# Attention and two feed-forward layers on one core: the second layer's second product of batches 2 and 3 from seven block products for eight, and due times shifted by kind of step and stage

## The chip, the cores and the metric

The kernel runs on one core of one Trainium2 chip. The metric is the device time of one execution in microseconds (us). Before the change the median of three timed runs is 1192.38 us (1186.67, 1192.38 and 1195.06).

## The reference

Attention with normalised queries and keys over 4 batches, 12 heads, 448 positions, head size 64; its output, put together to 1792 tokens by 768, goes through two feed-forward layers, each 768 to 2048 and back to 768, all in float32:

```
attn = softmax(rmsnorm(q) @ rmsnorm(k).T / 8) @ v
x = attn as [1792, 768]
h = x @ w_in;    x = (silu(h)) @ w_out          # first layer
h = x @ w2_in;   out = (relu(h) ** 2) @ w2_out  # second layer
```

## The kernel before, in words

The engines are named as in the profile: PE multiplies matrices, DVE, ACT and POOL work elementwise, SP issues the DMAs.

**Precision.** A float32 operand is split into an upper part in PE's fast format (a cast, kinds of step ending in `_hi`) and the rest (a subtraction, `_lo`). Each product is three matmuls: upper by upper, and the two of upper by lower. The casts stand at L523 (ACT) and L525 (DVE), the subtractions at L532 (DVE or POOL).

**Second layer** (`layer2`). It runs over two halves, each two batches: 896 tokens. In each half a loop over eight groups `fg` of 256 of the 2048 hidden features; one pass is called a slot here. The slot's first product, 768 to 256, is made from seven block products for eight (`seven`): the input halves B11 to B22 are combined beforehand (T1 to T4, B21, tiles `raw`, `yb`, `xb`, `part`), the weights too (w0, a22, z, v_, tiles `w` and `v`). Each of the products P1 to P7 is 9 matmuls of 448 columns (L1075) into a bank of the rings "t" (3 banks) or "pv" (1). DVE adds them up (`plus`, L1090) in the four buffers of ring `g`; ACT applies relu (L1338), DVE, ACT or POOL the square (L1344, L1346), and the result is split into `gh` and `gl`. The four blocks of it are named by (feature block, batch): (0,0), (0,1), (1,0), (1,1).

The second product takes 7 chunks of 128 tokens by two halves of 384 outputs. Each of these 14 is 6 matmuls of 384 columns (L1367) into a bank of ring "s", which has four; then ACT copies the bank into `total` in the first slot (L1388) or DVE adds it (L1394, "accumulate" below), tile `gg` in the profile. After the last slot each chunk is stored.

**What sets the order.** A planner (`Plan`) records all steps with each engine's cost for them, lists them by a simulated run forward, takes a due time for each from a run backward, and repeats this 8 times (`schedule`); between steps that could start at the same time the earlier due time goes first. Every engine then issues its steps in the order found. In half 1 (the second half, batches 2 and 3) the weights of the first product come ready split from DRAM (`w<-su`, `sw`, `sz`, `sv`, `v<-sa`, L927), each 768 KB (`sa` 384 KB). In the trace half 0 has its slots up to about 937 us, its accumulates to about 985 us beside the start of half 1, which ends with the kernel.

Of the kernel before, what the change touches and what calls it, by code (L numbers as in the profile page):

```python
# [8 lines left out]
F32 = mybir.dt.float32  # L9
# [6 lines left out]
P = 128  # L16
# [5 lines left out]
NQ = 4  # L22
# [6 lines left out]
SEVEN = (1,)  # L29
SEGS = [(h, n) for h in range(2) for n in range(NQ)]  # L30
# [81 lines left out]
AHEAD = 25.0  # L112


class Plan:
# [233 lines left out]
    def schedule(self):  # L349
# [7 lines left out]
        while todo:  # L357
            n = todo.pop()
            e = at[n]
            t, xfer, _ = steps[n].on[e]  # L360
            due[n] -= t + (xfer or 0.0) + LAG[e]
            for m, timed in self.pre[n]:
                due[m] = min(due[m], due[n])
                seen[m] -= 1
                if not seen[m]:
                    todo.append(m)
        best = None
        got = [None]
        for _ in range(ROUNDS):
# [4 lines left out]
            due = [-x for x in late]  # L374
# [14 lines left out]
def kernel(  # L389
# [674 lines left out]
    def seven(x, w, at, finish):  # L1064
# [36 lines left out]
        plus(u3, u2, p7)  # L1101
        p4 = psum("t")
# [5 lines left out]
        p5 = psum("t")  # L1108
        product(p5, z, 0, "T1")
        plus(u3, u3, p5)  # L1110
        finish(1, 1, u3)
        plus(u2, u2, p5)
# [201 lines left out]
    def layer2():  # L1314
# [3 lines left out]
        SLOT = 7 * PROD + TC * DOWN2  # L1318
        for half in range(2):
            t = half * NG * SLOT  # L1320
            x = second_x(half, ("end", t - 60.0), ("end", t - 20.0))
            total = sb([P, TC, DM], F32, "gg", 1, "yp")
            for fg in range(NG):
                f0, f1 = 2 * fg, 2 * fg + 1
                at = ("end", t)
# [5 lines left out]
                gl = sb([P, 2, 2 * S], FR, "gl", 1, "yp")  # L1331

                def finish(fi, bi, g, src=None, gh=gh, gl=gl):

                    k = slice(bi * S, (bi + 1) * S)
# [6 lines left out]
                    def square(e):  # L1342
# [5 lines left out]
                    step("square", at, {**any_t(S), **act_t(S)}, square, writes=[g])  # L1348
                    split(
                        ("h_hi", "h_lo"), at, lambda: gh.ap[:, fi, k], lambda: gl.ap[:, fi, k], lambda: g.ap,  # L1350
                        [g], [(gh, (fi, bi)), (gl, (fi, bi))],
                    )

                seven(x, w, ("end", t), finish)
                t += 7 * PROD

                for tc_ in range(TC):
                    bs = range(tc_ * P // S, ((tc_ + 1) * P - 1) // S + 1)
                    for nh in range(2):
                        pt = psum("s")  # L1360

                        def products(e, gh=gh, gl=gl, wo=wo, tc_=tc_, pt=pt, nh=nh):
                            n = 0
                            for fi in range(2):
                                _, _, wh, wl = wo[fi]
                                for w_, g in ((wh, gh), (wl, gh), (wh, gl)):
                                    nc.tensor.matmul(  # L1367
                                        pt.ap[:, :NH],
                                        g.ap[:, fi, tc_ * P:(tc_ + 1) * P],
                                        w_()[:, 0, nh * NH:(nh + 1) * NH],  # L1370
                                        start=(n == 0),
                                        stop=(n == 5),
                                    )
                                    n += 1

                        step(
                            "down2", ("end", t), pe_t(DOWN2 / 2), products,
                            reads=[z for w in wo for z in w[:2]]
                            + [(z, (fi, bi)) for z in (gh, gl) for fi in range(2) for bi in bs],
                            writes=[pt],  # L1380
                        )

                        def o(tc_=tc_, nh=nh, total=total):
                            return total.ap[:, tc_, nh * NH:(nh + 1) * NH]

                        if fg == 0:
                            step(
                                "acc", ("end", t), act_t(NH), lambda e, o=o, pt=pt: nc.scalar.copy(o(), pt.ap[:, :NH]),  # L1388
                                reads=[pt], writes=[(total, (tc_, nh))],
                            )  # L1390
                        else:
                            step(
                                "acc", ("end", t), dve_t(NH),
                                lambda e, o=o, pt=pt: nc.vector.tensor_tensor(o(), pt.ap[:, :NH], o(), ALU.add),  # L1394
                                reads=[pt], writes=[(total, (tc_, nh))],
                            )
                        t += DOWN2 / 2
                    if fg == NG - 1:

                        r0 = tc_ * P  # L1400
                        while r0 < (tc_ + 1) * P:
                            g_, t0_ = divmod(r0, CP)
                            r1 = min((tc_ + 1) * P, (g_ + 1) * CP)
# [3 lines left out]
                                lambda e, total=total, tc_=tc_, r0=r0, r1=r1, b_=b_ + 2 * half, c_=c_, t0_=t0_:  # L1407
                                engine(e).dma_start(
                                    out.rearrange("(b t c) e -> b c t e", b=B, c=NCH)[b_, c_, t0_:t0_ + r1 - r0, :],
                                    total.ap[r0 - tc_ * P:r1 - tc_ * P, tc_, :]),  # L1410
                                reads=[(total, (tc_, nh)) for nh in range(2)],
                            )
                            r0 = r1

# [51 lines left out]
```

## Time and profile before

| what | us |
|---|---|
| median of 3 timed runs | 1192.38 |
| lowest and highest of them | 1186.67, 1195.06 |
| the profiled execution, its own time | 1184.83 |
| its span, first to last instruction | 1183.0 |
| mean granted TensorE clock of the span, share of full speed | 0.998 |

The profiled execution is a fourth one. Its span is the part that the views show; 1.83 us lie around it. Busy times are unions of the instructions' times; a matmul's end is modelled, so matmuls overlap each other in the rows, and their pace is read from one start to the next.

### The profile page before, as it was taken

How to read it: one execution, taken by the hardware profiler on the slowest of the kernel's cores; microseconds unless marked ns; L12 is line 12 of the kernel's file. 1: busy time of each engine (PE TensorE's matmuls, PEld its weight loads, DVE VectorE, ACT ScalarE, POOL GpSimd, SP SyncE). 2: the span in 40 equal slices, each digit the busy share in tenths (PEclk: the TensorE clock that was granted, in tenths of full speed). 3: DMA queues.
4: the chain of work that ended last, by engine and by line, in shares of the span. 5: the costliest groups of instructions: out<-in, count | busy, mean ns of one | idle time of the engine just before them, and what ended most of it. 6: DMA issues, size and time to landing. Idle time of an engine off the chain costs nothing.

```text
span 1183.0 us, 18930 instructions
## 1 busy us (share of the span) xinstructions
PE 1156.8 (98%) x6888; PEld 1035.5 (88%) x6888; DVE 921.4 (78%) x1612; ACT 551.3 (47%) x1154; POOL 239.4 (20%) x445
## 2 busy tenths in 40 slices
PE   5999999999999999999999999999999999999998
PEld 3777777778899999999999999899999989999997
DVE  7999999987999999965689898789887843555544
ACT  5999999874443334422325262544333423111111
POOL 3566676531000010000001020011131300000000
PEclk9999999999999999999999999999999999999999
DMA  7455557639998888732247649888768694444443
GB/s 171 86 78 90 90 91 102 96 63 204 298 285 271 251 276 289 228 110 63 82 172 228 240 153 359 268 298 310 262 245 293 191 322 154 147 147 147 149 170 122
DMA packets 136700, 224.86 MB, mean 190 GB/s; under 512 B 31392, under 2 KB 102048, under 8 KB 136608
## 3 DMA queue, kind: packets, MB, share of 16 engines
q1 hardware_dynamic: 136608, 223.67, 63.0%
q8 instruction: 54, 0.88, 0.4%
q14 instruction: 38, 0.31, 0.1%
HBM read 149.32 MB, written 74.31 MB: 189 GB/s over the span
## 4 chain that ended last, share of the span: by engine, by line
PE 91%; DVE 5%; DMA 3%; issue 1%; SPq 0%; ACT 0%; DVEq 0%; ACTq 0%
PE s L1164 19%; PE s L1367 18%; PE t L1075 18%; PE t L988 7%; PE t L712 7%; PE pv L1075 7%; PE pv L761 6%; PE s L685 6%; PE t L632 2%; DMA raw<-in_moe_w_in_dram 1%; DMA w<-sz 1%; DVE w L532 1%; DMA qk<-in_k_dram 0%; DVE g L1090 0%; DVE W L903 0%
## 5 line engine op out<-in xcount | busy, mean ns | idle before, releaser
L1164 PE MATMUL s<-gg,w 128*128 128x448 f32 x1152 | 238.8, 365 | 0.8 <-DVE gg L532 0.7
L1164 PEld LDWEIGHTS s<-gg,w 128*128 128x128 f32 x1152 | 216.2, 188 | 18.8 <-DVE gg L532 1.4
L1367 PE MATMUL s<-w,gh 128*128 128x384 f32 x896 | 227.7, 334 | 0.7 <-DVE gg L1394 0.7
L1367 PEld LDWEIGHTS s<-w,gh 128*128 128x128 f32 x896 | 162.3, 188 | 2.2 <-DVE gg L1394 1.1
L1090 DVE TENSOR_TENSOR g<-t,g 128x448 f32<-128x448 f32 x144 | 87.3, 620 | 93.1 <-ACT g L511 53.9
L1394 DVE TENSOR_TENSOR gg<-s,gg 128x384 f32<-128x384 f32 x196 | 107.0, 554 | 57.0 <-PE s L1367 56.6
L1367 PE MATMUL s<-w,gl 128*128 128x384 f32 x448 | 150.0, 335 | 0.9 <-DVE gl L532 0.8
L703 ACT ACTIVATE E<-s,mx 112x448 f32<-112x448 f32 x192 | 122.1, 647 | 20.6 <-ACT xf L511 13.0
L988 PE MATMUL t<-xb,w 128*128 128x448 f32 x576 | 119.2, 366 | 0.7 <-ACT g L1000 0.7
L988 PEld LDWEIGHTS t<-xb,w 128*128 128x128 f32 x576 | 108.0, 188 | 10.2 <-ACT g L1000 1.0
L523 ACT CAST w<-W 128x768 fp32r<-128x768 f32 (+1 forms) x73 | 54.5, 750 | 125.4 <-PE s L1164 46.5
L532 DVE TENSOR_TENSOR w<-W,w 128x768 fp32r<-128x768 f32 (+1 forms) x121 | 107.3, 896 | 6.8 <-ACT w L523 5.9
L696 DVE TENSOR_REDUCE mx<-s 112x1 f32<-112x448 f32 x192 | 107.4, 610 | 6.1 <-PE s L685 5.4
L712 PEld LDWEIGHTS t<-ident,E 112*112 112x112 f32 x768 | 73.8, 134 | 32.0 <-issue 14.6
L712 PE MATMUL t<-ident,E 112*112 112x112 f32 x768 | 95.3, 267 | 0.8 <-DVE T L648 0.4
L1367 PEld LDWEIGHTS s<-w,gl 128*128 128x128 f32 x448 | 84.1, 188 | 1.9 <-DVE gl L532 1.9
L761 PE MATMUL pv<-PT,vv 112*64 112x224 f32 x768 | 83.1, 359 | 0.0
L1075 PE MATMUL t<-yb,w 128*128 128x448 f32 x360 | 80.2, 372 | 2.4 <-DMA w<-sz 2.4
L1075 PE MATMUL t<-xb,w 128*128 128x448 f32 x360 | 79.9, 367 | 0.0
L511 ACT COPY g<-pv 128x448 f32<-128x448 f32 x24 | 12.7, 531 | 140.1 <-PE pv L1075 130.6
L1075 PEld LDWEIGHTS t<-yb,w 128*128 128x128 f32 x360 | 68.5, 191 | 8.5 <-DMA w<-sz 2.7
L685 PE MATMUL s<-T 64*112 64x448 f32 x576 | 73.1, 384 | 2.6 <-ACT T L641 1.9
(119 smaller groups left out, 1803.7 us busy)
## 6 DMA issues: line engine op xcount, KB each, us to landing
raw<-in_moe_w_in_dram SPq DMA_DIRECT2D x25, 768.0 KB
raw<-in_moe_w_out_dram SPq DMA_DIRECT2D x24, 512.0 KB
su<-w SPq DMA_DIRECT2D x16, 768.0 KB
w<-su SPq DMA_DIRECT2D x16, 768.0 KB
xf<-y SPq DMA_DIRECT2D x48, 224.0 KB
raw<-in_moe_w_out_dram SPq DMA_DIRECT2D x10, 768.0 KB
ki<-W SPq DMA_DIRECT2D x16, 384.0 KB
ko<-W SPq DMA_DIRECT2D x24, 256.0 KB
```

What stands on the lines that cost most here:

```text
L532: kind, when, any_t(n, rate), lambda e: engine(e).tensor_tensor(o(), a(), h(), ALU.subtract),
L685: nc.tensor.matmul(pts[j].ap[:CP, :S], T.ap[r, 0, a, c * CP:(c + 1) * CP], T.ap[r, 1, b_], start=(k_ == 0), stop=(k_ == 2),)
L696: lambda e, pt=pt, mx=mx: nc.vector.tensor_reduce(mx.ap, pt.ap[:CP, :S], AX.X, ALU.max, negate=True),
L703: lambda e, j=j, c=c, pt=pt, mx=mx, E=E: nc.scalar.activation(E.ap[:, j], pt.ap[:CP, :S], AF.Exp, bias=mx.ap, accum_out=sums.ap[:, j, c:c ...
L712: nc.tensor.transpose(pe.ap[:CP, m * CP:(m + 1) * CP], E.ap[:, j, m * CP:(m + 1) * CP], ident.ap)
L761: nc.tensor.matmul(pv.ap[j * D:(j + 1) * D, c2 * CT * CP:(c2 + 1) * CT * CP], vr.ap[:, j * NCH + m, :], pt.ap[:, j * NCH + m].rearrange("p ...
L988: nc.tensor.matmul(pt.ap[:, :S], w_()[:, c, :], x[c // HC].ap[:, a, c % HC, :], start=(c == 0 and n == 0), stop=(c == NC6 - 1 and n == 2),)
L1075: nc.tensor.matmul(pt.ap[:, :S], w_()[:, c0 + c, :], view(b, a, c)(), start=(start and c == 0 and k == 0), stop=(c == HC - 1 and k == 2), ...
L1090: lambda e: nc.vector.tensor_tensor(o.ap, pt.ap[:, :S], a.ap, ALU.add),
L1164: nc.tensor.matmul(pt.ap[:, :S], w_()[:, f, :], gg.ap[:, k, a, f, :], start=(f == 0 and n == 0), stop=(f == HQ - 1 and n == 2),)
L1367: nc.tensor.matmul(pt.ap[:, :NH], g.ap[:, fi, tc_ * P:(tc_ + 1) * P], w_()[:, 0, nh * NH:(nh + 1) * NH], start=(n == 0), stop=(n == 5),)
L1394: lambda e, o=o, pt=pt: nc.vector.tensor_tensor(o(), pt.ap[:, :NH], o(), ALU.add),
```

## The change

1. In half 1 the second product of the slots 0 to 6 (not the last) is made from seven block products for eight. Of the 896 tokens, 384 rows of batch 2 are paired with 384 of batch 3, in three pairs of 128 rows. The blocks A11, A12, A21, A22 are the results (1,1), (0,1), (1,0), (0,0). Sums S1 to S4 of them and their split are made in each slot (`sums`), and sums of the weights of the two feature blocks with their split (`weights`, tiles `V`, `xb`, `W`), for which 14 transfers of 384 KB load the weights once more. Per pair there are 7 products of 3 matmuls (`down`), each in a bank of ring "s", with one accumulate for each; the product 2 is added into the bank that held product 1, after that was read. The remaining 128 rows go as before (12 matmuls). Two more sums, U2 and P7, are kept (tiles `xf`), and before the last slot's second product 15 additions (`join`) put the results together.
2. In those slots `seven` makes P5 ahead of P4, so that A11 is there first.
3. In half 1's last slot the chunks are taken in another order.
4. A table DUE shifts due times by the kind of step and the stage: of the first layer ("seg0", "seg1"), of the second ("end0", "end1"), and of steps that belong to none ("now").

```diff
+SEVEN2 = (1,)
+DUE = {
+    "end0": {"acc": -10.5, "down2": 0.25, "keep_parts2": -6.25, ...
...
+        moved = [DUE.get(stage(s), {}).get(s.kind, 0.0) for s in steps]
+        due = [d + x for d, x in zip(due, moved)]
...
-            due = [-x for x in late]
+            due = [x - y for x, y in zip(moved, late)]
...
-    def seven(x, w, at, finish):
+    def seven(x, w, at, finish, fifth=False):
...
+        if fifth:
+            p5 = psum("t")
+            product(p5, z, 0, "T1")
+            plus(c21, u3, p5)
+            finish(1, 1, c21)
+            plus(u2, u2, p5)
+            c21 = u3
         p4 = psum("t")
...
+                sums = later is not None and fg < NG - 1
...
+                    if sums:
+                        later.sums(fi, bi, whole, at)
...
+                if sums:
+                    later.weights(f0, f1, at)
+                    t = later.down(gh, gl, wo, fg, t, DOWN2)
+                    continue
+                if later is not None:
+                    later.join(("end", t - 7 * PROD))
+                chunks = [tc_ * P for tc_ in range(TC)]
+                if later is not None:
+                    chunks = [(1 - m % 2) * (2 * S - LEFT) + m // 2 * P for m in range(2 * NPAIR)] + [LEFT]
...
+            if (fi, bi) == (0, 0):
+                less(A22, A21, A22, ALU.add)
+                put("S1", A22)
+                less(A22, A22, A11)
+                put("S2", A22)
+                less(A21, A11, A21)
+                put("S3", A21)
+            if (fi, bi) == (0, 1):
+                less(A12, A12, A22)
+                put("S4", A12)
...
+            ops = {
+                1: (raw(1, 1), given(1, 0)), 2: (raw(0, 1), given(0, 0)), 3: (summed("S4"), given(0, 1)),
+                4: (raw(0, 0), made("42", 0)), 5: (summed("S1"), made("13", 0)), 6: (summed("S2"), made("42", 1)),
+                7: (summed("S3"), made("13", 1)),
+            }
...
+            for n in (4, 5, 7, 1, 6, 3):
+                for m in range(self.npair):
+                    pt = psum("s")
+                    product(n, m, pt, True, t)
+                    t += DOWN2 / 4
+                    add_to(*into({1: "U2", 6: "U2"}.get(n, f"P{n}"), m), pt, fg == 0 and n != 6, ("end", t))
+                    if n == 1:
+                        product(2, m, pt, False, t)
+                        t += DOWN2 / 4
+                        add_to(*into("C11", m), pt, fg == 0, ("end", t))
```

**Places in the order.** The lines of the code move by the change: L1075 becomes L1089, L1090 L1104, L525 L539, L532 L546, L1367 L1436, L1394 L1452; L1558 are the new products' matmuls, L1490 the sums S1 to S4, L1519 the sums of weights.

DVE in a slot of half 1, before (rows of one whole slot):

```order
L1090 TENSOR_TENSOR g<-t,g 128x448 x3
L525 CAST gh<-g 128x448
L532 TENSOR_TENSOR gl<-g,gh 128x448
L525 CAST gh<-g 128x448
L532 TENSOR_TENSOR gl<-g,gh 128x448
L1090 TENSOR_TENSOR g<-t,g 128x448 x3
L525 CAST gh<-g 128x448
L1394 TENSOR_TENSOR gg<-s,gg 128x384 x2
L532 TENSOR_TENSOR gl<-g,gh 128x448
L1394 TENSOR_TENSOR gg<-s,gg 128x384 x12
```

And now, the middle of a slot, from the additions of P4 and P3 on:

```order
L1104 TENSOR_TENSOR g<-t,g 128x448 x2
L1490 TENSOR_TENSOR g<-g 128x384
L546 TENSOR_TENSOR gl<-g,gh 128x64
L539 CAST part<-g 128x384
L1490 TENSOR_TENSOR g<-g 128x384
L546 TENSOR_TENSOR part<-g,part 128x384
L1452 TENSOR_TENSOR gg<-s,gg 128x384 x3
L1490 TENSOR_TENSOR g<-g 128x384
L546 TENSOR_TENSOR part<-g,part 128x384
L1452 TENSOR_TENSOR gg<-s,gg 128x384 x3
L1452 TENSOR_TENSOR xf<-s,xf 128x384 x7
L1452 TENSOR_TENSOR gg<-s,gg 128x384 x3
```

Between the last addition of P3 and the accumulates there now stand the sums S1, S3 and S2 with the splits of S1 and S3, and the accumulates are 23 for 14.

PE in the same slot, before (from the first product's last matmuls):

```order
L1075 MATMUL t<-xb,v 128x448 x9
L1075 MATMUL pv<-xb,w 128x448 x9
L1075 MATMUL t<-xb,w 128x448 x9
L1075 MATMUL t<-part,w 128x448 x9
L1367 MATMUL s<-w,gh 128x384 x2
L1367 MATMUL s<-w,gl 128x384
```

And now (`t<-xb,w` is P5, `t<-xb,v` P4, `t<-part,w` P3; `s<-xb,gh` begins product 4, `s<-xb,part` are products 5 and 7):

```order
L1089 MATMUL t<-xb,w 128x448 x9
L1089 MATMUL pv<-xb,w 128x448 x9
L1089 MATMUL t<-xb,v 128x448 x9
L1089 MATMUL t<-part,w 128x448 x9
L1558 MATMUL s<-xb,gh 128x384
L1558 MATMUL s<-W,gh 128x384
L1558 MATMUL s<-xb,gl 128x384
...
L1089 MATMUL pv<-raw,w 128x448 x9
L1558 MATMUL s<-xb,part 128x384 x18
```

The next slot's P1 (`pv<-raw`) now stands between product 4 and product 5 of this one. In slot 0 it stands later, and product 5 follows product 4 at once. In the last slot P1's second half (`pv<-xb`) now comes last of the seven, right behind P3, and the second product follows it.

PE at the turn from half 0 to half 1, before (`pv<-raw` is half 1's first P1, `t<-yb` its first P6):

```order
L1367 MATMUL s<-w,gl 128x384
L1075 MATMUL pv<-raw,w 128x448 x9
L1367 MATMUL s<-w,gh 128x384 x2
L1367 MATMUL s<-w,gl 128x384
L1367 MATMUL s<-w,gh 128x384 x2
L1367 MATMUL s<-w,gl 128x384
L1075 MATMUL t<-yb,w 128x448 x9
```

And now:

```order
L1436 MATMUL s<-w,gl 128x384
L1089 MATMUL t<-yb,w 128x448 x9
L1436 MATMUL s<-w,gh 128x384 x2
L1436 MATMUL s<-w,gl 128x384
L1436 MATMUL s<-w,gh 128x384 x2
L1436 MATMUL s<-w,gl 128x384
L1089 MATMUL pv<-raw,w 128x448 x9
```

P1 and P6 have changed places. From the end of half 0's last P3 to P6 there stood 42 matmuls of the second product and P1; now 78 matmuls of the second product stand there.

## Rows read from the trace of the kernel before

**Rows 1.** The page: span, and busy time of each engine.

```profile
span 1183.0 us, 18930 instructions
PE 1156.8 (98%) x6888; PEld 1035.5 (88%) x6888; DVE 921.4 (78%) x1612; ACT 551.3 (47%) x1154; POOL 239.4 (20%) x445
```

**Rows 2.** Waits of PE, whole span: total us, times, longest.

```profile
PE t L632 <- POOL y L611: 11.4, 1, 11.4
PE t L1075 <- DMA w<-sz: 2.4, 1, 2.4
...
PE s L1367 <- DVE gg L1394: 0.7, 1, 0.7
PE s L1164 <- DVE gg L532: 0.7, 1, 0.7
```

**Rows 3.** Windows of two slots: length, busy PE, PEld, DVE, ACT, POOL, clock, DMA.

```profile
985.20:1012.80 27.60, 27.60 (x150) 26.45 (x149) 13.72 (x25) 5.96 (x11) 1.16 (x1) 1.00 0.46 157
1122.90:1150.46 27.56, 27.56 (x149) 26.41 (x148) 14.19 (x26) 5.47 (x10) 1.17 (x1) 1.00 0.47 158
```

**Rows 4.** Timeline of that second slot: start, duration, engine, line.

```profile
1128.47 2.01 PE L1075 MATMUL t<-xb,v 128*128 128x448 f32 x9
...
1130.32 2.02 PE L1075 MATMUL pv<-xb,w 128*128 128x448 f32 x9
...
1142.49 0.33 PE L1367 MATMUL s<-w,gl 128*128 128x384 f32 x1
...
1143.01 0.33 PE L1367 MATMUL s<-w,gl 128*128 128x384 f32 x1
...
1143.38 0.56 DVE L1394 TENSOR_TENSOR gg<-s,gg 128x384 f32<-128x384 f32 x1 [0.48 <-PE s L1367]
```

**Rows 5.** Timeline of half 0's last slot: accumulates end to end.

```profile
941.92 1.47 DVE L1394 TENSOR_TENSOR gg<-s,gg 128x384 f32<-128x384 f32 x3
...
942.52 0.62 PE L1367 MATMUL s<-w,gh 128*128 128x384 f32 x2 [0.75 <-DVE gg L1394]
```

**Rows 6.** Timeline of the slot of rows 4: from a sum to a split.

```profile
1129.23 2.11 DVE L1090 TENSOR_TENSOR g<-t,g 128x448 f32<-128x448 f32 x3 [5.55 <-ACT g L511]
...
1131.38 0.58 ACT L1338 ACTIVATE g<-g 128x448 f32<-128x448 f32 x1 [2.18 <-DVE g L1090]
...
1131.99 0.58 ACT L1344 ACTIVATE g<-g 128x448 f32<-128x448 f32 x1
...
1132.60 0.39 DVE L525 CAST gh<-g 128x448 fp32r<-128x448 f32 x1 [1.25 <-ACT g L1344]
1133.03 0.63 DVE L532 TENSOR_TENSOR gl<-g,gh 128x448 fp32r<-128x448 f32 x1
```

**Rows 7.** Groups by line, 700 to 1183 us: count, busy us, mean ns.

```profile
L1394 DVE TENSOR_TENSOR gg<-s,gg 128x384 f32<-128x384 f32 x196 | 107.0, 554 | 57.0 <-PE s L1367 56.6
...
L1033 DVE TENSOR_TENSOR W<-W 128x384 f32<-128x384 f32 x13 | 7.1, 547 | 0.0
```

**Rows 8.** Timeline of PE at the turn of the halves.

```profile
935.19 2.02 PE L1075 MATMUL t<-part,w 128*128 128x448 f32 x9
937.05 0.52 PE L1367 MATMUL s<-w,gh 128*128 128x384 f32 x2
...
945.18 2.10 PE L1075 MATMUL pv<-raw,w 128*128 128x448 f32 x9 [0.31 <-DMA w<-sw]
...
950.75 3.50 PE L1075 MATMUL t<-yb,w 128*128 128x448 f32 x9 [2.41 <-DMA w<-sz]
```

**Rows 9.** Timeline of SP's queue there.

```profile
938.92 0.64 SPq L927 DMA_DIRECT2D w<-sz  x1
```

**Rows 10.** Windows there, columns as in rows 3; the last but two is the clock.

```profile
951.00:953.00 2.00, 2.00 (x6) 1.79 (x7) 0.00 (x0) 0.00 (x0) 0.00 (x0) 0.50 1.02 397
```

**Rows 11.** Timelines beside POOL's work, near 775 us.

```profile
774.72 1.01 POOL L532 TENSOR_TENSOR v<-W,v 128x384 fp32r<-128x384 f32 x1
...
775.36 0.85 DVE L532 TENSOR_TENSOR gl<-g,gh 128x448 fp32r<-128x448 f32 x1
```

**Rows 12.** The same in the slot of rows 4.

```profile
1137.58 1.17 POOL L532 TENSOR_TENSOR gl<-g,gh 128x448 fp32r<-128x448 f32 x1 [26.38 <-DVE gh L525]
...
1138.18 0.56 DVE L1394 TENSOR_TENSOR gg<-s,gg 128x384 f32<-128x384 f32 x1 [0.30 <-PE s L1367]
```

More of the change, by code (lines that the diff above doesn't have):

```diff
@@ L1107, in seven @@
         finish(0, 0, c11, p1)
[L1108 to L1112, printed above, removed]
+        if not fifth:
+            p5 = psum("t")
+            product(p5, z, 0, "T1")
+            plus(u3, u3, p5)
+            finish(1, 1, u3)
+            plus(u2, u2, p5)
         p3 = psum("t")
@@ L1355, in layer2 @@
+                    if sums:
+                        later.sums(fi, bi, whole, at)
+                seven(x, w, ("end", t), finish, sums)
                 t += 7 * PROD
-                for tc_ in range(TC):
-                    bs = range(tc_ * P // S, ((tc_ + 1) * P - 1) // S + 1)
+                if sums:
[4 more added lines that the diff above has]
+                    later.join(("end", t - 7 * PROD))
@@ L1359, in layer2 @@
+                chunks = [tc_ * P for tc_ in range(TC)]
+                if later is not None:
+                    chunks = [(1 - m % 2) * (2 * S - LEFT) + m // 2 * P for m in range(2 * NPAIR)] + [LEFT]
+                for tc_, c0 in enumerate(chunks):
                     for nh in range(2):
                         pt = psum("s")
[L1362 to L1374, printed above, removed]
@@ L1380, in layer2 @@
                             writes=[pt],
                         )
[L1383 to L1396, printed above, removed]
+                        accumulate(total, tc_, nh, pt, fg == 0, t)
@@ L1413, in layer2, with plain, products @@
                             r0 = r1
+    def plain(gh, gl, wo, c0, pt, nh):
+        def products(e):
+            n = 0
+            for fi in range(2):
+                _, _, wh, wl = wo[fi]
+                for w_, g in ((wh, gh), (wl, gh), (wh, gl)):
+                    nc.tensor.matmul(
+                        pt.ap[:, :NH], g.ap[:, fi, c0:c0 + P], w_()[:, 0, nh * NH:(nh + 1) * NH],
+                        start=(n == 0), stop=(n == 5),
+                    )
+                    n += 1
+        return products
@@ new lines, in accumulate, with add_to @@
+    def accumulate(total, tc_, nh, pt, first, t):
+        add_to(lambda: total.ap[:, tc_, nh * NH:(nh + 1) * NH], (total, (tc_, nh)), pt, first, ("end", t))
+    def add_to(o, k, pt, first, at):
+        if first:
+            step("acc", at, act_t(NH), lambda e: nc.scalar.copy(o(), pt.ap[:, :NH]), reads=[pt], writes=[k])
+        else:
+            step(
+                "acc", at, dve_t(NH), lambda e: nc.vector.tensor_tensor(o(), pt.ap[:, :NH], o(), ALU.add),
+                reads=[pt], writes=[k],
+            )
```

151 lines of the change are left out of this document (137 added, 14 removed).

## The prediction

> **What bounds the kernel now.** I read the page first: PE is busy 1156.8 us of a span of 1183.0 us, DVE 78% of it [rows 1]. Then the list of PE's waits, to see whether anything but PE's own work sets the time: apart from 11.4 us at the start, which the change does not touch, the longest wait is 2.4 us at the turn of the halves, and those on DVE are 0.7 us each [rows 2]. So a matmul that goes is time saved, as long as DVE and ACT keep up. The windows of two slots of half 1 show the room for that: 27.56 us a slot, PE busy all of it, DVE 14.19 us, POOL 1.17 us, at a granted clock of 1.00 [rows 3].
>
> **The change part by part.** *Matmuls that go.* Three matmuls of 384 columns take 0.52 us from start to start (1142.49 to 1143.01) [rows 4], 0.173 us each. A slot's second product has 84 of them before. After, it has 3 pairs x 7 products x 3 = 63, and 12 for the remaining 128 rows, so 75. Nine fewer in 7 slots are 63, and 63 x 0.173 = 10.9 us. The slot falls by 1.56 us to 26.0 us.
>
> *DVE's load.* The accumulates go from 14 to 23 a slot. One lasts 554 ns [rows 7], but three end to end take 1.47 us [rows 5], so that the next starts (1.47 - 0.555) / 2 = 0.46 us after the last. An addition of 448 columns takes 0.61 to 0.62 us and three of them 2.11 us [rows 6]; a sum of 384 lasts 547 ns [rows 7]; a split of 448 is 0.39 us for the cast and 0.63 us for the subtraction [rows 6], which I scale to 0.35 and 0.55 us for 384. At this pace a slot needs 23 x 0.46 = 10.6 us for accumulates, 6 x 0.54 = 3.2 for the additions of the first product, 6 x 0.5 = 3.0 for sums, about 4.3 for splits: 21 us of 26.0. At full durations it is about 24.4 us. Either fits, so what counts is when things are ready.
>
> *One slot walked through.* Time 0 is the end of P3 on PE; DVE starts 0.2 us after the last matmul's start plus pace (1143.01 + 0.173 to 1143.38) [rows 4], PE 0.05 us after DVE's end (942.47 to 942.52) [rows 5], ACT and DVE 0.03 to 0.04 us after each other [rows 6]. DVE adds P3 from 0.2, makes S1 at 0.74, casts it, makes S3, and ends S1's lower part at 2.7. PE runs product 4 to 1.56 and the next P1 to 3.42 (P1 is 1.85 us, 1128.47 to 1130.32 [rows 4]); product 5 needs S1's lower part at 3.42 plus two matmuls. It has 0.7 us to spare. DVE accumulates product 4 from 2.6 to 4.1, makes S2, and ends S3's lower part at 5.0; product 7 begins at 5.0 and wants it with its third matmul at 5.3. From there on 20 accumulates at 0.46 us each stand against a product of 0.52 us each; the ring of four banks never runs out. S2's lower part and S4 are POOL's, 1.1 us each; they end at about 7 and 8.3, wanted at 8.2 and 11.3. So a slot of 26.0 us is just possible. The best is 0; the worst, with accumulates that start only every 0.555 us, gives a slot of 27.8 us in the same walk, since each bank then comes late. I take 0.2 us a slot for the six slots 1 to 6, near the lower end because rows 5 show the pace: +1.2 us.
>
> *Slot 0.* Here product 5 follows product 4 with no P1 between: due at 1.56, its third matmul at 1.9, S1's lower part is there at 2.7. I take a wait of 1.0 us (bounds 0 and 2.7, all of the chain). The accumulates are ACT's copies here, and DVE has the splits of the input as well.
>
> *Last slot.* The first chunk now is of batch 3 and needs (0,1), which comes from P3; between them stands only P1's second half, 1.85 us. From P3's end: 0.2 to DVE, 0.62 addition, 0.58 relu, 0.58 square, 0.39 cast, 0.63 subtraction and the steps between make 3.1 us [rows 6]. That is 1.3 us late for the third matmul's operand less two matmuls' time: +1.1 us (0 to 1.3). The 15 additions of `join`, 547 ns each, lie beside 13 us of the first product.
>
> *The turn of the halves.* PE waited there 0.31 and 2.41 us for `w<-sw` and `w<-sz`, and the 9 matmuls behind took from 950.75 to about 954.1 instead of 1.85 us [rows 8]; the granted clock of 951 to 953 is 0.50, the lower of its levels (1.2 of 2.4 GHz), after the engine had stood still [rows 10]. Together 4.2 us. `w<-sz` was issued at 938.92 [rows 9] and landed some 11.8 us later. Now 78 matmuls x 0.173 = 13.5 us stand between P3's end (937.05) and P6, which puts P6 at 950.6: just when the weights landed. SP's queue holds the same transfers in nearly the same order. I take 3.5 us back (bounds 0 and 4.2).
>
> *The rest.* The 14 transfers more, 5.4 MB, lie in half 1, where the DMA share is 0.47 [rows 3]: nothing. The due times reorder DVE, ACT and SP from the first layer on, PE there only by small swaps. The waits left for them to gain are the 0.7 us ones [rows 2]; they can make as many new ones. I take 0, bounds -2 and +6.
>
> *Sum,* against the profiled execution of 1184.83 us: -10.9 + 1.2 + 1.0 + 1.1 - 3.5 = -11.1 us, so 1173.7 us. The median of the three runs, 1192.38, lies 7.6 us higher; the same difference gives 1181.3 us. The three runs spread over 8.4 us, so about 1% (11.9 us, below 1180.5) is what a measurement can tell from no change.
>
> **A rule weighed.** POOL works longer now, beside DVE's sums. A subtraction of DVE that ran into one of POOL's took 0.85 instead of 0.63 us [rows 6, 11], while an accumulate beside POOL kept its 0.56 us [rows 12]. The Trainium skill (SBUF — State Buffer, "Who interferes with whom") says that a DVE instruction with two SBUF inputs and a GpSimd instruction that reads SBUF shut each other out for the whole instruction, and that one with a single SBUF input is free. The trace agrees on both, as far as these rows go: DVE started 0.35 us before POOL's end and lost 0.22. By the row an overlap costs 0.2 us, by the rule up to POOL's whole length; the rule is worked out as a rival below.
>
> **The rivals.** *All covers hold* (22%): no wait in slots 0 and 7, all 4.2 us back: -10.9 - 4.2 = -15.1, 1177.3 us. For it: PE hardly waited for DVE before, with DVE busy 78% of the span [rows 1, 2]. Against it: the waits of slot 0 and of the last slot come out of durations in rows 6.
>
> *Accumulates do not overlap* (17%): each starts only when the last has ended. A slot is then 27.8 us, 0.3 more than before: 6 x 0.3 - 1.6 + 1.0 (slot 0) + 1.1 - 3.5 = -1.2, 1191.2 us. For it: each now adds from a bank just filled, and 23 of them stand almost without a gap. Against it: the 1.47 us of rows 5. The Trainium skill (VectorE: DVE Perf Modes, "The DRAIN you can't avoid") says that the next operation does not start until the pipe is empty, and points to a section by which one that is not held starts earlier; the first would be this rival, rows 5 show the second.
>
> *POOL shuts DVE out* (6%), the slower side: S1's lower part, S2 and S3's lower part are in each slot's chain, and POOL subtracts close to them. If each waits out a POOL instruction of 1.15 us, a slot is 26.1 + 3.4 = 29.5 us, 1.9 more than before: 6 x 1.9 + 0.5 (slot 0) + 1.1 = 13.0 us, and if the turn then gains nothing either 1205.4 us. It loses from 1.56 us of waiting a slot on. For it: rows 11. Against it: 0.2 us there, and in the walk POOL's subtraction ends before S2 begins.
>
> *The due times cost elsewhere* (10%): DVE's order is another from the first layer on; eight new waits of the 0.7 us kind give +5.6: 1186.9 us. Nothing in the rows speaks for it but DVE's load.
>
> **How the numbers follow.** The forecast, 1181.3 us, has 45%; its own range is 1177 to 1186. It lies close to the bound of 1%: about 40% of it falls below, 0.18, and with the first rival 0.40 for faster by over 1%. Slower by over 1% is the third, 0.06. The rest is 0.54. The range reaches from 1175 (the first rival less the spread of the runs) to 1193 (the second, with the same).
>
> **What would show it.** In the changed profile: PE's matmuls 63 fewer; windows of slots 2 to 6 of 26.0 to 26.4 us with DVE at 20 to 23 us; a wait of PE for a split of 0.5 to 1.2 us once in slot 0 and once in the last; no wait for `w<-sz` above 0.5 us and a clock of 1.00 there. It is wrong if slots take over 27 us (look whether accumulates start every 0.46 us, or whether subtractions beside POOL last over 1 us), if PE waits for `xf` or `part` inputs after the turn, or if waits of 1 us appear in the first layer.

## The result, and the profile after

The changed kernel's time is 1172.48 us (median of six runs, 1171.87 to 1175.94). Six runs of the kernel before, the three known ones and three taken beside it, have a median of 1185.89 us. The ratio is 0.9883, 95% interval 0.9844 to 0.9921: faster by 1.2%, below the range that was forecast.

The profiled execution took 1172.46 us, 12.4 less than that of before. The change of its span, 1183.0 to 1170.6, falls into four stretches; their borders are the starts of P3 (`t<-part` x9) in half 0's last slot and in half 1's slots.

| stretch | before | after | change | forecast |
|---|---|---|---|---|
| start to half 0's last P3 | 935.19 | 933.48 | -1.7 | 0 |
| from there to slot 0's P3 | 33.61 | 28.55 | -5.1 | -3.5 |
| seven slots | 192.78 | 185.75 | -7.0 | -8.7 |
| last slot and end | 21.42 | 22.82 | +1.4 | +1.1 |
| sum | 1183.0 | 1170.6 | -12.4 | -11.1 |

(After, the last slot's P3 stands one product of 1.86 us earlier in the order, which is put right here.) Against its own reference, the profiled execution, the forecast was off by 1.2 us; what went wrong is how it was carried over to the median. The first experiment shows that.

The page, answering [rows 1]: 63 matmuls fewer, PE as full as before, DVE at 84%.

```profile
span 1170.6 us, 19174 instructions
...
PE 1147.3 (98%) x6825; PEld 1022.6 (87%) x6825; DVE 986.7 (84%) x1737; ACT 577.7 (49%) x1205; POOL 298.1 (25%) x487
```

Waits of PE, answering [rows 2]. The wait for `w<-sz` is gone; in its place are one for `gh` in the last slot and two in slot 0, for ACT's copy `gg` and for `part`.

```profile
PE t L646 <- POOL y L625: 11.7, 1, 11.7
...
PE s L1436 <- DVE gh L539: 1.0, 1, 1.0
PE s L1558 <- ACT gg L1449: 1.0, 1, 1.0
...
PE s L1558 <- DVE part L546: 0.3, 1, 0.3
```

Windows of two slots, answering [rows 3] (length, busy PE, PEld, DVE, ACT, POOL, clock, DMA): 26.13 and 26.12 us for 27.6, DVE 21.7 us as forecast (21).

```profile
1060.11:1086.24 26.13, 26.13 (x139) 24.83 (x139) 21.70 (x44) 8.96 (x16) 7.14 (x6) 1.00 0.58 197
1086.24:1112.36 26.12, 26.12 (x139) 24.82 (x139) 21.69 (x44) 8.96 (x16) 7.15 (x6) 1.00 0.50 178
```

DVE in one of these slots, answering [rows 4 to 7]; P3's last matmul is followed at 1071.26 by product 4, the time 0 of the prediction's walk.

```profile
1071.46 0.62 DVE L1104 TENSOR_TENSOR g<-t,g 128x448 f32<-128x448 f32 x1 [0.89 <-PE t L1089]
1072.00 0.55 DVE L1490 TENSOR_TENSOR g<-g 128x384 f32<-128x384 f32 x1
...
1073.34 0.55 DVE L546 TENSOR_TENSOR part<-g,part 128x384 fp32r<-128x384 f32 x1
1073.81 1.48 DVE L1452 TENSOR_TENSOR gg<-s,gg 128x384 f32<-128x384 f32 x3
...
1075.67 0.55 DVE L546 TENSOR_TENSOR part<-g,part 128x384 fp32r<-128x384 f32 x1
1076.14 1.48 DVE L1452 TENSOR_TENSOR gg<-s,gg 128x384 f32<-128x384 f32 x3
```

S1's lower part ends at 1073.89, 2.63 us after time 0 (walk: 2.7), S3's at 1076.22, 4.96 after it (walk: 5.0). Three accumulates take 1.48 us, so each starts about 0.47 us after the one before it.

The turn, answering [rows 8 to 10]: PE, then SP's queue, then the window (the clock is the last but two).

```profile
933.48 2.02 PE L1089 MATMUL t<-part,w 128*128 128x448 f32 x9
...
949.86 2.02 PE L1089 MATMUL t<-yb,w 128*128 128x448 f32 x9
```

```profile
933.70 0.94 SPq L941 DMA_DIRECT2D w<-sz  x1
```

```profile
951.00:953.00 2.00, 2.00 (x13) 1.90 (x12) 1.56 (x4) 0.64 (x2) 0.00 (x0) 1.00 0.95 349
```

P6 starts without a wait, and the granted clock stays at the higher of its levels. But `w<-sz` goes out 1.64 us before P3's matmuls are through (933.48 + 1.86), where before it went out 1.87 us behind. The prediction had SP's queue as it was.

### The profile page after: what moved, and what is told of

It reads as the page before. It is cut to its first block, busy times and chain, and to the rows that moved or that the text cites. A ratio compares the mean times of both kernels' runs of the same rounds, so it can differ in the third digit from the quotient of the medians.

```text
span 1170.6 us, 19174 instructions
## 1 busy us (share of the span) xinstructions
PE 1147.3 (98%) x6825; PEld 1022.6 (87%) x6825; DVE 986.7 (84%) x1737; ACT 577.7 (49%) x1205; POOL 298.1 (25%) x487
## 4 chain that ended last, share of the span: by engine, by line
PE 88%; DVE 7%; DMA 3%; issue 1%; ACT 1%; SPq 0%; DVEq 0%; ACTq 0%
PE s L1186 18%; PE t L1089 16%; PE s L1436 12%; PE t L1002 7%; PE t L726 7%; PE pv L1089 7%; PE pv L775 6%; PE s L1558 6%; PE s L699 6%; PE t L646 2%; DVE w L546 1%; DMA raw<-in_moe_w_in_dram 1%; DVE g L1104 1%; DMA qk<-in_k_dram 0%; DMA v<-sa 0%
## 5 line engine op out<-in xcount | busy, mean ns | idle before, releaser
L1436 PE MATMUL s<-w,gh 128*128 128x384 f32 x560 | 142.7, 335 | 1.0 <-DVE gh L539 1.0
L1104 DVE TENSOR_TENSOR g<-t,g 128x448 f32<-128x448 f32 x144 | 86.9, 618 | 58.6 <-PE t L1089 53.3
L1452 DVE TENSOR_TENSOR gg<-s,gg 128x384 f32<-128x384 f32 x196 | 102.9, 550 | 28.2 <-PE s L1436 27.9
L1002 PEld LDWEIGHTS t<-xb,w 128*128 128x128 f32 x576 | 108.1, 188 | 8.9 <-issue 0.3
L546 DVE TENSOR_TENSOR w<-W,w 128x768 fp32r<-128x768 f32 (+1 forms) x118 | 103.7, 885 | 5.4 <-ACT w L537 4.0
L1436 PEld LDWEIGHTS s<-w,gh 128*128 128x128 f32 x560 | 101.4, 188 | 2.8 <-DVE gh L539 1.4
L1436 PE MATMUL s<-w,gl 128*128 128x384 f32 x280 | 93.9, 335 | 0.6 <-DVE gl L546 0.6
L1367 ACT ACTIVATE g<-g 128x448 f32<-128x448 f32 x48 | 27.7, 579 | 131.3 <-DVE g L1104 130.9
L1089 PE MATMUL t<-xb,w 128*128 128x448 f32 x360 | 80.1, 367 | 0.0
L1089 PE MATMUL t<-yb,w 128*128 128x448 f32 x360 | 79.1, 367 | 0.0
L1089 PEld LDWEIGHTS t<-xb,w 128*128 128x128 f32 x360 | 67.4, 188 | 6.3 <-DVE g L1104 0.4
L1089 PEld LDWEIGHTS t<-yb,w 128*128 128x128 f32 x360 | 67.4, 188 | 5.5
```

The costliest lines, as they stand in the source:

```text
L546: kind, when, any_t(n, rate), lambda e: engine(e).tensor_tensor(o(), a(), h(), ALU.subtract),
L1002: nc.tensor.matmul(pt.ap[:, :S], w_()[:, c, :], x[c // HC].ap[:, a, c % HC, :], start=(c == 0 and n == 0), stop=(c == NC6 - 1 and n == 2),)
L1089: nc.tensor.matmul(pt.ap[:, :S], w_()[:, c0 + c, :], view(b, a, c)(), start=(start and c == 0 and k == 0), stop=(c == HC - 1 and k == 2), ...
L1104: lambda e: nc.vector.tensor_tensor(o.ap, pt.ap[:, :S], a.ap, ALU.add),
L1436: nc.tensor.matmul(pt.ap[:, :NH], g.ap[:, fi, c0:c0 + P], w_()[:, 0, nh * NH:(nh + 1) * NH], start=(n == 0), stop=(n == 5),)
L1452: "acc", at, dve_t(NH), lambda e: nc.vector.tensor_tensor(o(), pt.ap[:, :NH], o(), ALU.add),
```

## The experiments

### The same two kernels profiled again

No edit, for either kernel.

> The kernel before, unchanged, profiled once more. Theory: its six timings lie between 1181.7 and 1195.1 us while those of the changed kernel lie within 4 us, because at the turn of the halves PE waits for a transfer (2.41 us for the weights z in the first profile) that lands earlier or later from run to run; then another profile of 1184.83 us plus or minus d shows d at that wait and at the slow matmuls behind it, and everything from the second slot of half 1 on takes the same time within 0.3 us. Rival: the spread lies in the start (the 11.4 us wait and the loading) or evenly over the span; then the turn is 5.7 us over its nominal time again and d is found elsewhere. A profile within 1 us of 1184.83 tells nothing on this.

> The changed kernel once more, unchanged. Theory (the timings of any of these kernels fall into two groups some 8 us apart, by whether the first layer's matmuls of 448 columns come every 0.2026 us or every 0.2067 us from some stall on; neither is the change's doing): its timings lie near 1172 us in part and up to 1181 in part, and if the profile shows the slower pace from a point in the first layer on, its excess over 1172.46 us is 0.0192 times the stretch from there to 728 us. Rival (the changed kernel has shed the slower group, which belongs to before's stall at the turn): no timing over 1176 us.

The second profile of before took 1190.17 us, that of the changed kernel 1178.77. Windows of 100 us in the first layer, where PE does nothing but matmuls of 448 columns: before, before again, changed, changed again.

```profile
400.00:500.00 100.00, 100.00 (x495) 92.69 (x494) 92.79 (x156) 42.31 (x70) 7.43 (x6) 1.00 0.80 258
```

```profile
400.00:500.00 100.00, 100.00 (x486) 90.81 (x485) 91.59 (x155) 42.14 (x70) 7.49 (x6) 1.00 0.77 257
```

```profile
400.00:500.00 100.00, 100.00 (x495) 92.70 (x494) 88.66 (x144) 39.50 (x64) 6.17 (x4) 1.00 0.80 262
```

```profile
400.00:500.00 100.00, 100.00 (x486) 90.81 (x485) 87.08 (x141) 39.00 (x63) 6.17 (x4) 1.00 0.77 258
```

PE is busy all the time at a granted clock of 1.00 in each, and yet it makes 495 matmuls in two of them and 486 in the other two (one that reaches over a border is counted). From start to start they take 0.2027 or 0.2067 us in the mean: 199, 207, 202, 203, 202 ns over and over, give or take 1 ns, or 207, 207, 206. In both of the longer profiles the longer pace sets in behind a stall of PE between 302 and 309 us and holds to the end of the first layer (in the changed kernel to 703 us). The other two have a stall there too, and keep the shorter pace. From the first matmul of the first layer's second product to its last, 424.47 us became 432.37 before, 425.62 became 432.98 with the change. A difference of this size is what the prediction carried over. The second theory's formula gives 7.6 us for the stretch that ends at 703 us; the profile is 6.3 us longer, with a slot 0 that is 1.0 us shorter than in the first. My theory for `before` was wrong: the turn's wait was 2.4 us again, only its matmuls were not slow this time (granted clock 1.00 there), which gave back 1.2 us.

The timings agree with two groups, though no timed run has a trace: of 73 of the kernel before, 54 lie between 1179.1 and 1186.7 and 19 between 1188.3 and 1195.1. Two of the three runs that the prediction had are of the upper group. Its share differs from set to set: 13 of 28, 4 of 31, 0 of 8. The changed kernel has both too: in its second set four at 1170.7 to 1172.1, two at 1178.8 and 1179.2. The lower four against the eight of before taken beside them (1181.3 to 1185.3): medians 1171.5 and 1183.2, 11.7 us apart. The groups are not sharp: in the traces of other experiments below the longer pace sets in at 488, 596 and 655 us, with a smaller part of the 8 us each, and in the changed kernel's first profile it holds for some 36 us between 696 and 743 us.

### Each half of the change alone

```diff
-SEVEN2 = (1,)
+SEVEN2 = ()
```

> The table of due times alone, with the second product of half 1 from all eight block products as before. Theory (the due times win back the turn of the halves, 4.7 us, and 1.9 us in the two layers, and cost nothing in the old slots): 6.6 us less than before in a profile of each, so about 1178 us, with no wait for w<-sz. Rival 1 (they give only the turn): about 1180 us, the first layer as long as before. Rival 2 (they win back the turn only because 78 matmuls of the second product stand ahead of P6 there, and they cost elsewhere, +5.6 us): 1185 us or more. The nine matmuls a slot more are in it in any case, so that none of the 10.9 us of the matmuls shows.

```diff
-DUE = {
...
+DUE = {}
```

> The seven products and what belongs to them alone, with the table of due times empty. Theory: the 10.9 us of matmuls, less the new waits (2.1 us in slot 0, 1.0 in slot 1, 1.5 in the last, some 0.5 in the others), so 5.8 us less than before plus what the turn is then worth: P6 stands 12.3 us behind P3 and its weights land some 13.7 us behind it, so a wait of about 1.4 us and slow matmuls behind it stay, 1 us less than before. About 1178 us. Rival 1 (the due times do nothing that counts): 1172.5 us, as the whole change. Rival 2 (the due times are what makes the slots fit, and without them S1's and S3's lower parts or POOL's splits come late in each slot): 1 us a slot and more, 1184 us or over, with waits of PE for part in slots 2 to 6.

The due times alone: median 1185.81 us, ratio to before 1.0002 (0.9975 to 1.0030). The seven products alone: median 1172.61 us, ratio 0.9897 (0.9862 to 0.9933), the same as the whole change. Both theories for the table fall; rival 1 of the second is what happened. Of the first, rival 2 has the number (1185 us or more), though not its reason. With the table alone the turn is mostly won (29.55 us from P3 to P3), but half 0's last P3 starts at 940.53, 5.3 us later than before. One of the new waits is in the second layer's first slot:

```profile
747.34 2.09 PE L1089 MATMUL t<-part,w 128*128 128x448 f32 x9 [1.60 <-DVE g L1104]
```

The longer pace from 655 us on, some 1.5 us, is in the 5.3 us as well, and so is a wait of 1.5 us for ACT (`g`); the rest was not taken apart. Without the table the turn is won too, 28.63 us, although P1 still comes ahead of P6:

```profile
932.73 2.02 PE L1083 MATMUL t<-part,w 128*128 128x448 f32 x9
```

```profile
932.96 0.95 SPq L935 DMA_DIRECT2D w<-sz  x1
```

`w<-sz` goes out before P3 ends here as well. So neither the table nor the exchange of P1 and P6 is needed; something had held SP's queue before.

```diff
-    "now": {"ident": 1.5, "swap_pools": 1},
...
```

The lines "seg0" and "seg1" go as well.

> The whole change, but due times are shifted in the second layer alone, not in the first and not for the steps that belong to neither. The order at the turn and in half 1 is that of the whole change. Theory (1.9 us come from the first layer's order): 1174.4 us, half 0's last P3 starts 1.7 us later than in the whole change, near 935.2. Rival (those 1.9 us are the second layer's, or differ from run to run): 1172.5 us, P3 near 933.5.

1177.73 us, ratio 0.9927 (0.9898 to 0.9956): 5 us lost, more than either said, and in another place, the second layer's first slot:

```profile
PE pv L1086 <- ACT g L1364: 4.3, 1, 4.3
```

Half of the table costs 5 us, the whole of it nothing, none of it nothing. That shifts of one layer fit only the order that the others made would explain this; no run shows it.

### What held SP's queue at the turn

In the trace of before POOL has one subtraction of 5.37 us in the stretch ahead of the turn; the next of the same form takes 1.15.

```profile
930.74 5.37 POOL L1216 TENSOR_TENSOR xf<-xf 128x448 f32<-128x448 f32 x1 [14.11 <-DMA xf<-y]
938.77 1.15 POOL L1216 TENSOR_TENSOR xf<-xf 128x448 f32<-128x448 f32 x1 [2.66 <-DVE xb L532]
```

DVE meanwhile (three of its rows):

```profile
932.74 0.62 DVE L532 TENSOR_TENSOR gl<-g,gh 128x448 fp32r<-128x448 f32 x1
933.27 1.82 DVE L532 TENSOR_TENSOR w<-W,w 128x768 fp32r<-128x768 f32 x2
935.01 1.01 DVE L1394 TENSOR_TENSOR gg<-s,gg 128x384 f32<-128x384 f32 x2
```

And SP, its waits from 925 to 945 us and its queue:

```profile
SPq L1208 <- POOL xf L1216: 6.2, 2, 5.5
```

```profile
929.58 0.32 SPq L927 DMA_DIRECT2D v<-sa  x1
936.14 1.27 SPq L1208 DMA_DIRECT2D xf<-y  x3
937.50 0.38 SPq L927 DMA_DIRECT2D w<-sw  x1
```

DVE runs without a gap on SBUF tiles until 935.01 and then turns to accumulates, which read one operand from PSUM; POOL ends 1.10 us after that, about its usual length. SP waits 5.5 us for the buffer, and `w<-sw` and `w<-sz` stand behind. In the second profile of before POOL's subtraction takes 5.27 us and ends 1.10 us after the same turn of DVE. The Trainium skill (SBUF — State Buffer, "Who interferes with whom") says that a DVE instruction with two SBUF inputs contends with a GpSimd instruction that reads SBUF, over ports that are an exclusive lock, and that one with at most one SBUF input is free of this outside the two-port modes, which a cast can enter; the 5.37 us agree, on the side that the prediction's rival had not looked at. In the changed kernel SP's wait for this tile in the same 20 us is 1.0 us:

```profile
SPq L1230 <- POOL xf L1238: 1.0, 1, 1.0
```

```diff
         self.span, start, at, order = self.schedule()
+        sums = [n for n in order if self.steps[n].kind == "y_sum" and at[n] == "pool" and start[n] > 925]
+        for n in sums[:1]:
+            dve = [m for m in order[:order.index(n)] if at[m] == "dve"]
...
+            order.remove(n)
+            order.insert(order.index(dve[-6]), n)
+            at[n] = "dve"
```

> The kernel before, with one instruction changed: the subtraction xf that POOL made at 930.74 to 936.11 us (5.37 us where others of the same kind take 1.15) is made by DVE, one place between its subtractions near 931.5; nothing else moves on any engine. Theory (the turn's stall began there: DVE's run of subtractions kept POOL's back, its buffer came free late, SP stood behind the load into that buffer, and the weights w<-sw and w<-sz went out 3.5 us late): w<-sz goes out before half 0's last P3 ends, PE waits neither for sw nor for sz, and the time from that P3 to the next falls by 3.5 to 4.7 us, so about 1178.5 us where the profile of before had 1184.83 (a slow first layer put aside). Rival 1 (the weights' buffers are free only when the products before have read them, so w<-sz goes out at the same time): no change within 0.5 us. Rival 2 (the order of P1 and P6, or the 78 matmuls ahead, win the turn back): no change either, since PE's order is untouched.

The turn, from P3 to P3, is 28.50 us (940.39 to 968.89): 5.1 less than in the first profile of before, 3.9 less than in the second, and equal to the changed kernel's. PE has no wait there for `sw` or `sz`, P6 none at all, and SP's wait for POOL is gone:

```profile
940.39 2.02 PE L1082 MATMUL t<-part,w 128*128 128x448 f32 x9
...
952.32 2.02 PE L1082 MATMUL t<-yb,w 128*128 128x448 f32 x9
```

```profile
941.27 1.64 SPq L934 DMA_DIRECT2D w<-sz  x1
```

Its ten timings fall into 1176.9 to 1179.1 (five) and 1184.9 to 1187.2 (five, the profile among them, with the longer pace), so that the median, 1181.98, and the ratio, 0.9987 (0.9956 to 1.0018), hide a gain of about 4 us that each group shows against the same group of before beside it (27 from 1179.1 to 1184.8 and four from 1189.3 to 1190.9). Whether the edit has to do with there being five longer ones in ten is not shown. One instruction on another engine is worth the whole of the turn. Both rivals fall. That DVE's run is what holds POOL back is read from times, not tried by itself, but this trace has it once more: POOL's next subtraction takes 2.07 us and ends 1.09 us after DVE's turn to accumulates (940.76).

```profile
939.78 2.07 POOL L1223 TENSOR_TENSOR xf<-xf 128x448 f32<-128x448 f32 x1 [17.95 <-DMA xf<-y]
```

### The slots' margin

```diff
                 split(("h_hi", "h_lo"), at, h, l, lambda: of(t), [t], [hk, lk], L)
+                lower_part("h_lo", at, l, lambda: of(t), lambda: h().bitcast(F32), L, [t, hk], [lk])
```

> The changed kernel, with the lower parts of the sums S1 to S4 subtracted twice (the same values written again), so that four more subtractions of 384 columns are made in each of the seven slots, on DVE or POOL. Theory (what counts is when S1's and S3's lower parts are ready, with 0.7 and 0.3 us to spare in the walk of a slot, not DVE's load of 21.7 of 26.1 us): S1's lower part ends 0.5 us later, S3's 1.1 us later, so each of the slots 1 to 6 waits 0.6 to 0.9 us at product 7, 3.6 to 5.4 us in all, and slot 0 0.5 us more. Rival 1 (the planner puts the second subtractions where there is room, on POOL): under 1 us in all. Rival 2 (DVE is close to the bound, its real capacity about what it has to do): each slot grows by the full 2.2 us, 15 us in all.

1188.44 us. The slots 2 to 5 take 27.58 us in the mean (from P3 at 1023.88 to P3 at 1134.19), 1.45 more than 26.13; PE waits for `part` in each of seven slots:

```profile
PE s L1559 <- DVE part L546: 6.3, 7, 1.3
```

```profile
1051.28:1079.04 27.76, 26.57 (x139) 24.82 (x138) 24.91 (x50) 10.39 (x20) 4.61 (x4) 1.00 0.51 192
1079.04:1106.44 27.40, 26.74 (x139) 24.75 (x138) 23.61 (x48) 9.41 (x18) 4.22 (x3) 1.00 0.50 181
```

So it is a wait for a split, as the theory has it, but the slot grows by about twice what it said, and the wait is at product 5, not at product 7. In the slot from 1079.04 the second subtraction of S1 stands behind three accumulates and ends 4.5 us after time 0, where the first ended at 2.63. DVE is busy 23.6 to 24.9 us of 27.4 to 27.8, not all of it, and the full 2.2 us of rival 2 are not reached. In every other slot, as in the one from 1051.28, the planner also put the next P1 behind product 5, so the size is not the subtraction's alone; some 6 us of the total lie ahead of half 1.

### The new waits of slot 0 and of the last slot

```diff
-                for tc_, c0 in enumerate(chunks):
+                for tc_, c0 in sorted(enumerate(chunks), key=lambda z: (z[1] == LEFT, -(z[0] % 2)) if later is not None else z[0]):
```

> The changed kernel, with the chunks of batch 2 first in half 1's last slot, so that its first matmuls need (0,0) and (1,0) and not what comes from P3. Theory (the wait of 1.0 us and the 1.55 us that the last slot takes over its matmuls' pace come from the chain P3, addition, relu, square, cast, subtraction): that wait goes, 1.2 to 1.5 us less than the changed kernel in the last slot. Rival (the joins on DVE, 15 additions, are what holds the slot, or the stores come later at the end): the wait moves to an accumulate or to the tail, within 0.5 us of the changed kernel.

```diff
-            step("acc", at, act_t(NH), lambda e: nc.scalar.copy(o(), pt.ap[:, :NH]), reads=[pt], writes=[k])
+            copy_step("acc", at, ("act", "dve"), o, lambda: pt.ap[:, :NH], NH, [pt], [k])
```

> The changed kernel, with the copies of the first slot's banks (half 0 and half 1) by ACT or DVE as the planner likes, not by ACT alone. Theory (slot 0 of half 1 loses 2.1 us because product 5 follows product 4 at once and ACT's copies free the banks of ring s late): the wait for ACT's copy, 1.0 us, goes, the one for S1's lower part, 0.3 us and the slow matmul behind it, stays: slot 0 is 0.8 to 1.2 us shorter. Rival (DVE's splits come later for the copies it takes): the wait moves to part, slot 0 no shorter.

In the first the last slot's wait is gone and the slot takes 21.32 us, 1.5 less, as the theory said. But the median is 1178.22 us: the planner's order is another everywhere, and the profile, 8.9 us longer than the changed kernel's, shows

```profile
PE t L1089 <- DVE g L1104: 2.5, 1, 2.5
PE s L1558 <- ACT gg L1449: 2.2, 1, 2.2
```

the first at the start of the second layer, the second in slot 0. It also runs at the longer pace from 488 to 721 us, worth 4.5 us, which is not the edit's price; the three shortest of its ten timings are 1174.0 to 1174.7 us. The second experiment (1177.37 us) has slot 0 longer, not shorter: 31.0 us from P3 to P3 (962.24 to 993.24), with 2.4 us of waiting for the copy. Its profile has the longer pace from 596 us on, and its shortest timings are 1175.8 to 1176.1 us. In the second profile of the changed kernel there is no such wait, and slot 0 takes 27.18 us, 1.16 more than its matmuls, against 28.16 in the first. ACT's copy waited for a transfer in the first:

```profile
967.46 2.40 ACT L1449 COPY gg<-s 128x384 f32<-128x384 f32 x6 [0.89 <-DMA v<-sa]
```

The copy does not read `v`; a store of half 0 out of the tile it writes is the likelier one, which was not tried. The wait is in one of the two profiles.

To be rid of the planner, the last three were made by moving steps of the finished order, which leaves every other instruction where it was. First, P1's second half ahead of P3 in the last slot, and batch 2's chunks first:

```diff
         self.span, start, at, order = self.schedule()
...
+        p3, p1b = pe[-2:]
...
+        head = [p1b] + of(p1b, -2, 11, 6, -1, 7) + [p3] + of(p1b, 8, 1, 9, 2, 10, 3, 4, 13, 14, 15)
...
+        order = order[:k] + head + rest[:3] + low + rest[3:]
```

> The changed kernel with its order kept word for word but for half 1's last slot: P1's second half goes before P3 there, and the second product takes the three chunks of batch 2 first. Theory (that slot's 1.55 us are the chain behind the block that is finished last, and the earlier try lost elsewhere only because the planner made another order of everything): PE does not wait there for over 0.3 us, 1.2 to 1.5 us less than the changed kernel. Rival (DVE's joins and accumulates hold the slot): the wait moves to an accumulate, under 0.5 us gained.

1171.91 us, no gain that the runs can tell; the wait is 0.83 for 0.98 us and has not moved to an accumulate either. The first matmul now needs the block (0,0), whose relu stands on ACT behind relu and square of the block before it:

```profile
1147.28 0.58 ACT L1381 ACTIVATE g<-g 128x448 f32<-128x448 f32 x1
1147.89 0.58 ACT L1387 ACTIVATE g<-g 128x448 f32<-128x448 f32 x1
1148.37 0.53 ACT L1381 ACTIVATE g<-pv 128x448 f32<-128x448 f32 x1
```

P1 was through at 1147.13, the relu (the third row) starts 1.2 us later: it is ACT's queue, which neither theory nor rival had. Second, the next P1 behind product 4 in slots 0 and 1:

```diff
+        for c in [n for n in order if self.steps[n].kind == "p1_copy" and start[n] > 960][:2]:
...
+            order.remove(n)
+            order.insert(k + 1, n)
```

> The changed kernel with its order kept but for two places of PE: in slots 0 and 1 of half 1 the next slot's P1 goes right behind product 4, as it stands in the slots 2 to 6. Theory (slots 0 and 1 lose 2.1 and 1.0 us because products 5 and 7 have too little in front of them): both come down to 26.1 to 26.3 us, 2.5 to 3 us less than the changed kernel in all. Rival 1 (the weights of that P1 have not landed, 7 us earlier than it stood): PE waits for w<-sw in slot 0, with the clock at its lower level behind it, nothing gained there. Rival 2 (ACT's copies of slot 0 free the banks too late whatever stands before): slot 0 keeps 1.0 us of its wait, slot 1 gains 0.9.

Rival 1: the weights are not there.

```profile
968.54 2.10 PE L1098 MATMUL pv<-raw,w 128*128 128x448 f32 x9 [2.52 <-DMA w<-sw]
```

Slot 0 takes 30.02 us; 1174.98 us in all. The clock, which the rival had at its lower level, is 1.00 from 967 to 975 us. In the order of the changed kernel P1 stands late enough in slot 0 not to wait for its weights. Slot 1 takes 26.97 us as before, although its P1 has gone forward: PE now waits 0.70 us for `part` at 1003.28 instead, so that moving P1 alone does not shorten it, and the theory falls.

> Both of these edits. Theory: they are 150 us apart and share no stretch, so their gains add: 3.7 to 4.5 us less than the changed kernel, near 1168.3 us where the first layer runs at its faster pace. Rival: as far as one of the two alone fails, its part is missing here too.

1172.59 us with both, and again 2.8 us of waiting for `w<-sw`, this time with a granted clock of 0.51 behind it (969 to 971 us) and a slot 0 of 31.84 us. None of the versions is faster than the changed kernel by more than its runs spread.

## Why the prediction was wrong

*The step that failed* is the last of the sum: "The median of the three runs, 1192.38, lies 7.6 us higher; the same difference gives 1181.3 us". It took a property of some executions for one of the kernel. The first layer's matmuls have two paces, 2.0% apart, worth 7.4 and 7.9 us in the pairs of profiles, and two of the three runs most likely had the longer one (they have no trace). Three more runs beside them brought before's median to 1185.89, and the later sets have 1182.4 to 1184.1. Without that step the forecast is 1173.7 us, against 1172.46 profiled and 1172.48 in the median; a range moved down by the same 7.6 would have held it. The profiled execution, 1184.83, lay below all three runs, and the three were spread over 8.4 us: the prediction saw both and made them a width of 1%, not a question.

That the sum of the terms came out so close is partly luck: the slots gave back 1.7 us less than forecast and the last slot 0.3, while the turn and the stretch ahead of it gave 3.3 more.

*Matmuls that go and the steady slots* were right: 10.6 us by the slots, 10.9 forecast. A slot of seven products without any wait takes 26.02 us (two of them in the trace of the seven products alone), so 7 x (27.54 - 26.02). The walk was right to 0.1 us. Slots 2 to 6 lose 0.1 us each and slot 1 loses 1.0, 1.5 together where 1.2 were forecast. The walk did not hold for slot 1: there too the next P1 stands late (997.18, behind 15 matmuls of products 5 and 7), which the places in the order give for slot 0 alone.

*Slot 0*: 1.0 us forecast, 1.2 in one profile and 2.1 in the other. The cause that was named, S1's lower part, is a wait of 0.3 us in the first profile, with slow matmuls around it; the wait for ACT's copy, 1.0 us, was not in the sum.

*Last slot*: 1.1 forecast, 1.4 measured. The prediction's own terms, 3.1 - 1.85 less two matmuls, give 0.9. The wait of 0.98 us is for the upper part at the first matmul, not for the lower one at the third: P3 is through at 1147.78, and DVE's addition starts 0.7 us later, not 0.2, behind a subtraction for another block.

```profile
1147.92 0.63 DVE L546 TENSOR_TENSOR gl<-g,gh 128x448 fp32r<-128x448 f32 x1
1148.46 0.62 DVE L1104 TENSOR_TENSOR g<-t,g 128x448 f32<-128x448 f32 x1
```

*The turn*: -3.5 forecast, -5.1 measured, and the reason was only half right. It counted matmuls ahead of P6 and took SP's issue as given. The transfer went out 3.5 us earlier by P3's end, because SP no longer waited 5.5 us for a POOL instruction. All of the 4.2 us came back; of the smaller waits there, which were not in the sum, the 0.75 us of [rows 5] went and 0.57 us for `gl` came.

*The rest*: 0 forecast, -1.7 measured ahead of half 1. It is not the table's, since without the table half 0's last P3 starts at 932.73, earlier still. The due times as such are worth nothing that was measured.

*The rivals*: accumulates overlap (0.47 us apart); how that rival's slot of 27.8 us follows from the rows is not worked out in the prediction. In the slots 2 to 6 DVE's accumulates and additions that started beside POOL kept their lengths, each with one input in PSUM. None of its sums or splits, with two inputs in SBUF, started while POOL computed, so *POOL shuts DVE out* was not met there, which is not the same as refuted. In the last slot it was: an addition of `join` takes 1.37 us for 0.54 beside one of POOL's.

```profile
1137.97 1.37 DVE L1610 TENSOR_TENSOR xf<-xf 128x384 f32<-128x384 f32 x1
```

```profile
1137.66 1.26 POOL L1610 TENSOR_TENSOR gg<-gg 128x384 f32<-128x384 f32 x1 [6.35 <-DVE gg L1610]
```

So an overlap can cost 0.8 us, not only the 0.2 that the prediction took from [rows 11]. (There DVE started 0.37 us before POOL's end, not 0.35; and the list behind [rows 2] has a wait for DVE of 0.8 us as well, not only of 0.7. Neither changes a sum.) "All covers hold" was too bright by the waits of slots 0, 1 and 7, and its 1177.3 us carries the same 7.6.

*Still open*: what decides the pace. In the four profiles of the two kernels it changed only at stalls of PE, and nothing in the traces tells one stall from another; in the profile with batch 2's chunks first it went back to the shorter one near 721 us with no step above 207 ns.

## What to carry to other kernels

Compare a profile with a median only after asking what differs between executions: count the matmuls of a stretch in which PE is full. Where a transfer is late, follow its queue back to the buffer it waits for; here one long instruction of POOL there was worth more than the order of the engine that waits. To test one cause in a planned kernel, move one step of the finished order: here each change of the planner's input moved much else as well.

## What was not expected of the hardware

A PE that is never idle, at a granted clock of 1.00, made 495 or 486 matmuls of 448 columns in 100 us, and kept to the one or the other for up to 430 us. And a subtraction of POOL took 4.2 us longer than its usual 1.15 beside eight back-to-back instructions of DVE, two casts among them, and ended only 1.10 us after them; it did not get in between.
